# Weight words of the first three chunks made on GpSimd, and a written-out order for the first two groups of a float64-weight attention + MoE kernel

## The chip, the cores and the metric

One core of a Trainium2 chip. The metric is the device time of one execution in microseconds, as the median of several runs. Engines are named as in the profile: PE (TensorE matmul), PEld (its weight load), DVE (VectorE), ACT (ScalarE), POOL (GpSimd), SP (SyncE, which here issues the loads).

## The reference

```python
scores = scale * q @ k.T                      # 2 x 8 heads, 768 tokens, 64 wide
scores = scores - slopes * dist, masked to 8 global and 96 local keys
a = exp(scores - max) / (sum + 1e-9)
x = (a @ v) as 1536 x 512
h = x @ w_in                                  # 512 x 2048, float64 weights
g = where(h > 0, h, exp(min(h, 0)) - 1)
y = g @ w_out                                 # 2048 x 512
out = max(y @ w1, y @ w2, y @ w3) @ w_out2    # 512 x 768, 768 x 512
```

The weights arrive as float64, so each is a pair of 32-bit words. Matmuls run in fp32r, with each operand split in a high part and a rest; a product is three matmuls (high by high, high by rest, rest by high).

## The kernel before, in words

**Attention steps.** `Windowed` treats (256-token group, head pair, 128-token half) as a step k. A step's parts are spread over the engines: the load of q and k of a pair (`load_pair`, L190, SP), the product of q with its scale on POOL (`scale_queries`, L198, 128x256), the score matmuls (`scores_pe`, L228), bias and minimum on DVE (`scores_dve`, L254), the exponential on ACT (`scores_act`, L275), the sums (`sums`, L237), the reciprocal (`recip`, L266) and the norm (`norm`, L288: two DVE instructions a step, one per head), the transposes (`turn_pe`, L304, `turn_act`, L315), the product with v (`values_pe`, L327) and its split into high and rest (`values_high`, L337 on ACT, `values_low`, L343 on DVE).

**Prologue.** `windowed` runs steps 0 to 15 in a loop in which step k's scores stand beside the transposes of k-2 and the values of k-3. `FILL` puts idle matmuls on PE (L762) behind the scores of some steps. `WLOAD` says behind which steps a weight chunk (1 MB: one 128-column block of w_in and the matching rows of w_out) is loaded (L422, SP). From step 8 (`CONV`) on, a generator `convert` adds one piece of weight conversion a step. Steps 16 and 17 stand behind the loop, written out, with the second half of the first product between them (`half`).

**Conversion of a chunk** takes six passes over 128x1024 words: `c_rebase` (L457, ACT) scales the upper word as a float, `c_low` (L461, DVE) takes the lower word's top bits, two `c_word` (L468, DVE) join them to an fp32 word, `c_high` (L476, ACT) casts to fp32r, `c_rest` (L481, DVE) subtracts that from the word. `parts` gives the chunk's tile.

**Groups.** `run` then goes through three blocks of 512 tokens; in each, 16 groups fc: product h = x by w_in (`product`, L674), the ELU (L694, L695 on ACT, L699 on DVE), the split of its result (`high`, L681 ACT; `low`, L686 DVE), and the product with w_out of the group before (`out_high`, L705, `out_low`, L713). In the first block each group also carries an attention step of the second token block and the conversion of the chunks to come. Every engine works in the program's order (`manual_schedule`); waits are on semaphores only. Later, POOL also subtracts words for the second layer (`w_split`, L510), beside DVE's word passes there (`w_word`, L500).

Of the kernel before, what the change touches and what calls it, by code (L numbers as in the profile page):

```python
# [12 lines left out]
F32 = mybir.dt.float32  # L13
# [5 lines left out]
ALU = mybir.AluOpType  # L19
# [19 lines left out]
BLOCKS = [512, 512, 512]  # L39
CONV = 8  # L40
EARLY = 28
WARM = 10
FILL = {1: 2, 2: 2, 8: 2, 9: 2, 10: 2, 11: 2, 12: 2, 13: 2}
WLOAD = 2, 5, 9, 13
CHUNKS = [(c, i) for c in range(NCC) for i in range(3)]
BEHIND = [(c, i) for c in range(NCC) for i in (0, 2)] + [(c, 1) for c in range(NCC)]
# [352 lines left out]
class Feed:  # L399
# [45 lines left out]
        while self.nl <= min(a + (6 if self.nl < 2 * NFC else 2), 2 * NFC + 4 * NJ - 1):  # L445
            self.w_load()

    def parts(self, c):

        if c in self.whole:  # L450
            return [(self.whole[c], slice(0, 2))]
        return [(self.wraw[j], j % 2) for j in (2 * c, 2 * c + 1) if j in self.wraw and c < NFC]

    def c_rebase(self, c):
        for r, _ in self.parts(c):
            a = r[..., 1].bitcast(F32)
            self.nc.scalar.activation(a, a, AF.Copy, scale=2.0 ** -112)  # L457

    def c_low(self, c):
        for r, _ in self.parts(c):  # L460
            self.nc.vector.tensor_scalar(  # L461
                r[..., 0], r[..., 0], 29, 1, op0=ALU.logical_shift_right, op1=ALU.bitwise_or
            )

    def c_word(self, c, n):
        v, op = ((3, ALU.logical_shift_left), (0x80000000, ALU.bitwise_and))[n]
        for r, _ in self.parts(c):
            self.nc.vector.scalar_tensor_tensor(  # L468
                r[..., 0], r[..., 1], v, r[..., 0], op0=op, op1=ALU.bitwise_or
            )  # L470

    def c_high(self, c):
        for r, h in self.parts(c):
            if c not in self.w:
                self.w[c] = self.wt.tile([P, 2, 2, 512], F32R, tag="w", name="w")
            self.nc.scalar.copy(self.w[c][:, h, 0], r[..., 0].bitcast(F32))  # L476

    def c_rest(self, c):
        for r, h in self.parts(c):
            w = self.w[c]  # L480
            self.nc.vector.tensor_tensor(  # L481
                w[:, h, 1], r[..., 0].bitcast(F32), w[:, h, 0].bitcast(F32), op=ALU.subtract
            )
        for d, k in ((self.whole, c), (self.wraw, 2 * c), (self.wraw, 2 * c + 1)):
            if c < NFC:
                d.pop(k, None)
# [275 lines left out]
            self.nc.tensor.matmul(t[:, 0:P], z, z, start=True, stop=True)  # L762


    def run(self, at, k, x=None, h0=None, aside=None):

        nc, ps = self.nc, self.ps
        nblk = len(BLOCKS)  # L770
# [4 lines left out]
        ysave = {}  # L775
        left = None
        for bi, n in enumerate(BLOCKS):
            prev = y = None
            for fc in range(NFC):
                tag = ("h", "S0")[fc % 2] if k >= len(at.steps) + 2 else "h"  # L780
                if h0 is None:
                    h = ps.tile([P, 512], F32, tag=tag, name="h")[:, 0:n]
                    self.product(h, self.w[fc][:, 0], x, n, order=BEHIND if bi == 0 else None)
                else:
                    h, h0 = h0[:, 0:n], None
# [15 lines left out]
                if not late:  # L801
                    at.turn_act(k - 1, nc.vector.tensor_copy)
                    if k % 2 == 0:
                        at.pair_pe(k - 2)
                    at.scores_dve(k)
                    e = self.elu_exp(h, n)
                    at.scores_act(k)
                    if k % 2 == 0:
                        at.pair_out(k - 2, nc.scalar.copy)
                else:  # L810
                    ahead = bi == 0 and fc == NFC - 1
                    behind = joint and due and (ahead or k == len(at.steps))
                    if ahead:
                        at.scores_dve(k)
                        at.scores_act(k)
                        at.sums(k)
                        at.recip(k)
                        at.norm(k)
                    e = self.elu_exp(h, n)
                    if joint:  # L820
                        at.due_out(due, nc.scalar.copy)
                        if not behind:
                            at.turn_pe(k - 1)
                    if bi == fc == 0:
                        at.turn_act(k - 2, nc.scalar.copy)
# [4 lines left out]
                sooner = bi == 0 and (fc == 0 or k % 2)  # L830
                if sooner:
                    self.elu_max(e, h)
                if bi == 0 and not ahead:
# [22 lines left out]
                gl = self.low(e, gh, n)  # L856
# [9 lines left out]
                if late and bi:  # L866
# [1 line left out]
                    at.sums(k)  # L868
                    at.recip(k)
                    at.norm(k)  # L870
                if k % 2 == 0 and bi == fc == 0:
                    at.pair_pe(k - 2)
                    at.pair_out(k - 2, nc.scalar.copy)
                left = None
                if k % 2 == 1:
                    at.scale_queries(k // 2 + 1)
# [8 lines left out]
                if k % 2 == 0 and not joint and bi + fc:  # L885
                    at.pair_pe(k - 2)
                    at.pair_out(k - 2, nc.scalar.copy)
                if aside and bi == 1 and fc == 2:
# [293 lines left out]
def windowed(tc, ctx, io, flag):  # L1182
# [5 lines left out]
    with tc.manual_schedule():  # L1188
# [10 lines left out]
        x = f.split_tiles()  # L1199

        def convert():
            f.c_rebase(0)
            f.c_low(0)
            yield
            f.c_word(0, 0)
            f.c_rebase(1)
            yield
            f.c_word(0, 1)
            yield
            f.c_high(0)  # L1210
            f.c_low(1)
            yield
            f.c_rest(0)
            yield
            f.c_word(1, 0)
            yield

        words = convert()
# [2 lines left out]
        for k in range(first):  # L1221
            e = k % 2
            at.load_values(k, True)
            if e == 0:
                at.load_pair(k // 2 + 3, True)
                at.scale_queries(k // 2 + 1)
            at.scores_pe(k, (("S0", "S1"), ("y0", "y1"))[e])
            if k in FILL:
                f.fill(at.ident, FILL[k])
            at.turn_pe(k - 2, tags[k % 3])  # L1230
            at.values_pe(k - 3)
            if k >= first - 2:
                f.product(h, f.w[0][:, 0], x, GRP, 0, (k - first + 2) * 6, 6)
            at.scores_dve(k, True)
            at.turn_act(k - 2, nc.scalar.copy)
            at.scores_act(k)
            at.values_high(k - 3, x)
            at.sums(k)
            at.recip(k - 1)
            at.norm(k - 1)  # L1240
            at.values_low(k - 4, x)
            if k >= CONV:
                next(words, None)
            if k in WLOAD:
# [13 lines left out]
        at.turn_act(k - 2, nc.scalar.copy)  # L1258
        at.values_high(k - 3, x)
        at.values_low(k - 4, x)  # L1260
        at.scores_pe(k, m=2)
        at.turn_pe(k - 1, tags[(k + 1) % 3])
        at.scores_dve(k, True)
# [124 lines left out]
```

## Time and profile before

| | before |
|---|---|
| median of 3 runs (range) | 543.22 us (542.96 to 543.47) |
| profiled execution, its own time | 542.19 us |
| its span in the profile | 540.4 us |
| PE busy | 530.7 us (98%) |
| DVE busy | 393.7 us (73%) |
| ACT busy | 288.0 us (53%) |
| POOL busy | 82.9 us (15%) |

The span is the time from the first to the last instruction in the profile; the execution's own time also has what lies around it. Busy time of PE counts a matmul from its start to its modelled end, and matmuls overlap, so the share is no measure of the work done. Shares over the whole span hide that the kernel has stages with different limits: the first 60 us hold the prologue and the first groups, on which the change bears.

### The profile page before, as it was taken

The numbers are of one execution on the slowest core, as the hardware profiler recorded it, in microseconds if no ns is written. First come the engines' busy times: TensorE is split into PE (matmuls) and PEld (weight loads), VectorE is DVE, ScalarE is ACT, GpSimd is POOL, SyncE is SP. The second block draws the span as 40 slices with busy tenths as digits, with TensorE's granted clock in tenths as the row PEclk, the third lists the DMA queues.
The fourth block names the chain that finished last, engine by engine and source line by source line (L and its number), as shares of the span: only waits on it lengthen the run. The fifth ranks groups of instructions, "written<-read, shape, count | busy, mean of one in ns | idle before, by whom it ended". The sixth has DMA issues, their size and how long they took to land.

```text
span 540.4 us, 7751 instructions
## 1 busy us (share of the span) xinstructions
PE 530.7 (98%) x2746; PEld 426.8 (79%) x2746; DVE 393.7 (73%) x828; ACT 288.0 (53%) x649; POOL 82.9 (15%) x89
## 2 busy tenths in 40 slices
PE   8999999999999999999999999999999999999995
PEld 6667787777777888888888888888888888888884
DVE  6889999999854444443567656787886989779883
ACT  5979877888845555554545655552157321224020
POOL 4220000000000000000000044321034410335000
PEclk9999999999999999999999999999999999999999
DMA  8929055442310111000000031331029301876014
GB/s 284 397 95 409 21 196 196 156 161 83 101 46 24 45 44 44 21 19 1 0 2 0 1 117 40 116 115 42 1 71 308 146 1 40 270 293 234 1 73 168
DMA packets 23455, 59.21 MB, mean 110 GB/s; under 512 B 2416, under 2 KB 2416, under 8 KB 23408
## 3 DMA queue, kind: packets, MB, share of 16 engines
q1 hardware_dynamic: 18368, 49.46, 26.5%
q10 hardware_dynamic: 5040, 9.18, 4.5%
q8 instruction: 24, 0.39, 0.3%
q14 instruction: 23, 0.19, 0.1%
HBM read 49.19 MB, written 9.44 MB: 108 GB/s over the span
## 4 chain that ended last, share of the span: by engine, by line
PE 91%; DVE 5%; ACT 3%; issue 0%; POOL 0%; ACTq 0%; POOLq 0%
PE h L674 26%; PE y L705 16%; PE y L713 8%; PE y L975 8%; PE y L1069 5%; PE y L674 5%; PE S L975 4%; PE TX L327 3%; PE TX L304 3%; PE S L228 3%; PE S L1069 2%; PE TX L975 2%; PE S L674 2%; PE h L975 2%; PE TX L1069 2%; ACT p L275 1%
## 5 line engine op out<-in xcount | busy, mean ns | idle before, releaser
L674 PE MATMUL h<-xh,w 128*128 128x512 f32 (+1 forms) x432 | 122.2, 387 | 0.2 <-ACT w L476 0.2
L705 PE MATMUL y<-gh,w 128*128 128x512 f32 x384 | 98.7, 399 | 0.1
L510 POOL TENSOR_TENSOR w<-wr,w 128x512 fp32r<-128x512 f32 x42 | 62.9, 1507 | 231.8 <-ACT w L509 220.5
L674 PEld LDWEIGHTS h<-xh,w 128*128 128x128 f32 x432 | 80.2, 188 | 17.9 <-ACT w L476 0.8
L705 PEld LDWEIGHTS y<-gh,w 128*128 128x128 f32 x384 | 69.7, 188 | 14.3 <-issue 0.5
L674 PE MATMUL h<-xl,w 128*128 128x512 f32 (+1 forms) x216 | 71.0, 386 | 0.0
L699 DVE SCALAR_TENSOR_TENSOR e<-e,h 128x512 f32<-128x512 f32 x48 | 32.9, 685 | 49.5 <-ACT e L695 49.4
L509 ACT CAST w<-wr 128x512 fp32r<-128x512 f32 x42 | 27.6, 663 | 63.4 <-DVE wr L500 51.1
L694 ACT ACTIVATE e<-h 128x512 f32<-128x512 f32 x48 | 28.7, 599 | 55.3 <-PE h L674 51.2
L275 ACT ACTIVATE p<-p,m 128x232 f32<-128x232 f32 (+1 forms) x96 | 44.9, 471 | 17.1 <-DVE m L254 16.9
L713 PE MATMUL y<-gl,w 128*128 128x512 f32 x192 | 51.6, 390 | 0.0
L500 DVE SCALAR_TENSOR_TENSOR wr<-wr 128x512 uint32<-128x512 uint32 x48 | 44.2, 921 | 7.5 <-ACT wr L492 6.0
L686 DVE TENSOR_TENSOR gl<-e,gh 128x512 fp32r<-128x512 f32 x48 | 33.1, 689 | 19.9 <-ACT gh L681 19.9
L674 PEld LDWEIGHTS h<-xl,w 128*128 128x128 f32 x216 | 40.4, 188 | 8.1 <-issue 0.2
L198 POOL TENSOR_SCALAR raw<-raw,qsc 128x256 f32<-128x256 f32 x24 | 16.8, 699 | 193.4 <-DMA raw<-qk 193.4
L975 PE MATMUL y<-t,w 128*128 128x512 f32 x180 | 42.7, 389 | 0.0
L713 PEld LDWEIGHTS y<-gl,w 128*128 128x128 f32 x192 | 36.0, 188 | 8.0 <-issue 0.3
L681 ACT CAST gh<-e 128x512 fp32r<-128x512 f32 x48 | 29.6, 616 | 23.5 <-DVE e L699 23.3
L468 DVE SCALAR_TENSOR_TENSOR wr<-wr 128x1024 uint32<-128x1024 uint32 (+1 forms) x36 | 39.8, 1120 | 0.4
L975 PEld LDWEIGHTS y<-t,w 128*128 128x128 f32 x180 | 33.8, 188 | 7.0
L695 ACT ACTIVATE e<-e 128x512 f32<-128x512 f32 x48 | 30.3, 632 | 1.5
L985 ACT CAST g<-m 128x512 fp32r<-128x512 f32 x18 | 10.9, 621 | 35.2 <-DVE m L1004 27.0
(155 smaller groups left out, 837.5 us busy)
## 6 DMA issues: line engine op xcount, KB each, us to landing
wr<-wa SPq DMA_DIRECT2D x14, 1024.0 KB, 6.9
wr<-wb SPq DMA_DIRECT2D x24, 512.0 KB, 4.6
v<-v SPq DMA_DIRECT2D x24, 256.0 KB, 2.8
part<-row ACTq DMA_DIRECT2D x24, 256.0 KB, 4.6
raw<-qk SPq DMA_DIRECT2D x16, 312.0 KB, 4.6
row<-part SPq DMA_DIRECT2D x12, 256.0 KB, 3.1
out<-rows ACTq DMA_DIRECT2D x11, 256.0 KB, 2.3
raw<-qk SPq DMA_DIRECT2D x8, 260.0 KB, 4.7
```

What stands on the lines that cost most here:

```text
L275: self.nc.scalar.activation(p[:, o], p[:, o], AF.Exp, bias=m[:, u:u + 1], scale=-1.0, accum_out=m[:, 2 + u:3 + u],)
L468: self.nc.vector.scalar_tensor_tensor(r[..., 0], r[..., 1], v, r[..., 0], op0=op, op1=ALU.bitwise_or)
L500: self.nc.vector.scalar_tensor_tensor(t, a, c, t, op0=op, op1=ALU.bitwise_or)
L510: nc.gpsimd.tensor_tensor(w[:, u, 1], v, w[:, u, 0].bitcast(F32), op=ALU.subtract)
L674: nc.tensor.matmul(out[:, o:n], w[:, part % 2, c * P:c * P + P], (xl if part == 2 else xh)[:, c, o:n], start=(c, part) == order[0], stop=( ...
L686: (engine or self.nc.vector).tensor_tensor(gl[:, 0:n], e[:, 0:n], gh[:, 0:n].bitcast(F32), op=ALU.subtract)
L695: self.nc.scalar.activation(e, e, AF.Exp, scale=-1.0)
L699: self.nc.vector.scalar_tensor_tensor(e, e, -1.0, h, op0=ALU.add, op1=ALU.max)
L705: self.nc.tensor.matmul(y[e][:, 0:n], w[:, a, e * P:e * P + P], g[0][:, 0:n], start=fc == 0 and a == 0, stop=False,)
L713: self.nc.tensor.matmul(y[e][:, 0:n], w[:, 0, e * P:e * P + P], g[1][:, 0:n], start=False, stop=fc == NFC - 1,)
L975: self.nc.tensor.matmul(out, w[:, u, i % 2, b + c * P:b + c * P + P], o[:, i // 2, c], start=c == i == 0, stop=c == 1 and i == 2,)
L1069: nc.tensor.matmul(o, t[:, a, r], w[:, u, b], start=u == k == 0, stop=u == 1 and k == 2,)
```

## The change

- `c_early` is new: on POOL, it makes the bottom bits of a chunk (a multiplication of the lower word by 2^-29 with a cap of 7, in place of a shift and an OR of 1) and the rebased upper word (a multiplication by 2^-112). `POOLED = {5: 0, 8: 1, 14: 2}` puts it at the end of steps 5, 8 and 14, for chunks 0, 1 and 2. `c_rebase` and `c_low` of these chunks are gone.
- `convert` is reordered: step 8 has the first word pass of chunk 0, step 9 its second, step 10 its cast and the first word pass of chunk 1, step 11 the rest of chunk 0, steps 12 to 14 nothing, step 15 the second word pass of the first half of chunk 1. The other half, the two half casts and the first half rest of chunk 1 stand among steps 16 and 17.
- `FILL` has no entries for steps 12 and 13 any more (two instructions each).
- `begin` is new: the first two groups of `run` in a written-out order. `run` then starts at the third.

```diff
-FILL = {1: 2, 2: 2, 8: 2, 9: 2, 10: 2, 11: 2, 12: 2, 13: 2}
+FILL = {1: 2, 2: 2, 8: 2, 9: 2, 10: 2, 11: 2}
+POOLED = {5: 0, 8: 1, 14: 2}
...
+    def c_early(self, c):
+        for r, _ in self.parts(c):
+            a = r[..., 1].bitcast(F32)
+            self.nc.gpsimd.tensor_scalar(
+                r[..., 0], r[..., 0], 2.0 ** -29, 7.0, op0=ALU.mult, op1=ALU.min
+            )
+            self.nc.gpsimd.tensor_scalar(a, a, 2.0 ** -112, 1.0, op0=ALU.mult, op1=ALU.mult)
...
+    def begin(self, at, k, x, h):
+        copy, n = self.nc.scalar.copy, BLOCKS[0]
+        at.load_values(k)
+        self.w_ahead(4)
+        at.turn_pe(k - 2, "y2")
+        at.scores_pe(k, m=2)
+        at.recip(k - 1)
+        at.norm(k - 1)
+        at.turn_pe(k - 1)
+        e = self.elu_exp(h, n)
+        self.elu_max(e, h)
+        h = self.ps.tile([P, 512], F32, tag="h", name="h")
+        self.product(h, self.w[1][:, 0], x, n, order=BEHIND)
+        at.turn_act(k - 2, copy)
+        at.scores_dve(k)
+        self.c_rest(1, 1)
+        gh = self.high(e, n)
+        at.turn_act(k - 1, copy)
+        at.scores_act(k)
+        at.sums(k)
+        self.c_word(2, 0)
+        prev = gh, self.low(e, gh, n)
+        at.pair_pe(k - 2)
+        e = self.elu_exp(h, n)
+        self.c_word(2, 1)
+        self.elu_max(e, h)
+        at.pair_out(k - 2, copy)
+        self.c_high(2)
...
         def convert():
-            f.c_rebase(0)
-            f.c_low(0)
-            yield
             f.c_word(0, 0)
-            f.c_rebase(1)
             yield
             f.c_word(0, 1)
             yield
             f.c_high(0)
-            f.c_low(1)
+            f.c_word(1, 0)
             yield
             f.c_rest(0)
             yield
-            f.c_word(1, 0)
+            yield
+            yield
+            yield
+            f.c_word(1, 1, 0)
             yield
...
             if k in WLOAD:
                 f.w_load()
+            if k in POOLED:
+                f.c_early(POOLED[k])
...
+        f.c_word(1, 1, 1)
+        f.c_high(1, 0)
+        f.c_high(1, 1)
         at.scores_pe(k, m=2)
...
         at.values_low(k - 2, x)
+        f.c_rest(1, 0)
...
-        f.run(at, first + 2, x, h, lambda: covered(nc, at.const, ni, flag))
+        begun = f.begin(at, k + 2, x, h)
+        f.run(at, first + 4, x, begun, lambda: covered(nc, at.const, ni, flag))
```

POOL's queue from the set-up to the second layer, before (`raw` is a pair's q and k, `wr` a weight chunk, `w` its converted form):

```order
L110 MEMSET qsc 64x1 x8
masks.py:197 MEMSET ident 128x128
masks.py:199 AFFINE_SELECT ident<-ident 128x128
L198 TENSOR_SCALAR raw<-raw,qsc 128x256 x24
L510 TENSOR_TENSOR w<-wr,w 128x512 x42
```

and now:

```order
masks.py:199 AFFINE_SELECT ident<-ident 128x128
L199 TENSOR_SCALAR raw<-raw,qsc 128x256 x4
L460 TENSOR_SCALAR wr<-wr 128x1024
L463 TENSOR_SCALAR wr<-wr 128x1024
L199 TENSOR_SCALAR raw<-raw,qsc 128x256 x2
L460 TENSOR_SCALAR wr<-wr 128x1024
L463 TENSOR_SCALAR wr<-wr 128x1024
L199 TENSOR_SCALAR raw<-raw,qsc 128x256 x3
L460 TENSOR_SCALAR wr<-wr 128x1024
L463 TENSOR_SCALAR wr<-wr 128x1024
L199 TENSOR_SCALAR raw<-raw,qsc 128x256 x15
L523 TENSOR_TENSOR w<-wr,w 128x512 x42
```

Two passes over a chunk stand behind the products of pairs 0 to 3, two behind pairs 4 and 5, two behind pairs 6 to 8; the products of pairs 4, 6 and 9 now wait for them.

DVE in step 11, from its reciprocal to the scores of step 12 (`p` is a step's probabilities, `m` its small numbers, `xl` the rest of x), before:

```order
L266 RECIPROCAL m<-m 128x2
L288 TENSOR_SCALAR p<-p,m 128x232 x2
L343 TENSOR_TENSOR xl<-TX,xh 128x128
L461 TENSOR_SCALAR wr<-wr 128x1024
L254 ISA p,m<-S_475,rel 128x232
```

and now:

```order
L267 RECIPROCAL m<-m 128x2
L289 TENSOR_SCALAR p<-p,m 128x232 x2
L344 TENSOR_TENSOR xl<-TX,xh 128x128
L492 TENSOR_TENSOR w<-wr,w 128x2x512
L255 ISA p,m<-S_477,rel 128x232
```

The bottom bits of chunk 1 have left; the rest of chunk 0, which stood in step 12, has taken their place.

DVE in the first group, from the end of its scores on (`e` is the ELU's tile, `h` the product, `gl` the rest of the group's result), before:

```order
L461 TENSOR_SCALAR wr<-wr 128x1024
L481 TENSOR_TENSOR w<-wr,w 128x2x512
L266 RECIPROCAL m<-m 128x2
L288 TENSOR_SCALAR p<-p,m 128x232 x2
L686 TENSOR_TENSOR gl<-e,gh 128x512
L468 SCALAR_TENSOR_TENSOR wr<-wr 128x1024 x2
L699 SCALAR_TENSOR_TENSOR e<-e,h 128x512
```

and now:

```order
L492 TENSOR_TENSOR w<-wr,w 128x512
L479 SCALAR_TENSOR_TENSOR wr<-wr 128x1024
L699 TENSOR_TENSOR gl<-e,gh 128x512
L479 SCALAR_TENSOR_TENSOR wr<-wr 128x1024
L712 SCALAR_TENSOR_TENSOR e<-e,h 128x512
L267 RECIPROCAL m<-m 128x2
L289 TENSOR_SCALAR p<-p,m 128x232 x2
```

The bottom bits of chunk 2 and half of the rest of chunk 1 have left, and the norm now stands behind the second group's ELU.

## Rows read from the trace of the kernel before

**Rows 1.** Busy us by stretch: PE, PEld, DVE, ACT, POOL, clock, DMA share, GB/s

```profile
10.00:20.00 10.00, 8.77 (x78) 5.52 (x78) 8.08 (x46) 8.90 (x39) 1.43 (x3) 1.00 1.04 404
20.00:30.00 10.00, 9.73 (x83) 6.88 (x82) 9.86 (x38) 10.00 (x32) 2.31 (x4) 1.00 0.84 321
...
100.00:120.00 20.00, 20.00 (x106) 15.96 (x105) 19.07 (x39) 16.02 (x35) 0.48 (x1) 1.00 0.56 195
```

**Rows 2.** Timeline of PE, first groups: start, length, line, operation, [idle before <-ended by]

```profile
43.84 0.68 PE L304 MATMUL TX<-ident,p 128*116 128x128 f32 x4 [0.37 <-DVE p L288]
...
53.10 0.50 PE L674 MATMUL h<-xh,w 128*128 128x512 f32 x1 [0.21 <-ACT w L476]
```

**Rows 3.** Timeline of DVE, steps 5 to 8, same columns

```profile
13.55 0.48 DVE L288 TENSOR_SCALAR p<-p,m 128x128 f32<-128x128 f32 x2
...
14.39 0.29 DVE L254 CUSTOM_DVE_ANT_0 p<-S,rel 128x128 f32<-128x128 f32 x1 [0.16 <-PE S L228]
...
15.43 0.17 DVE L266 RECIPROCAL m<-m 128x2 f32<-128x2 f32 x1 [0.53 <-ACT m L237]
15.63 0.59 DVE L288 TENSOR_SCALAR p<-p,m 128x232 f32<-128x232 f32 x2
...
17.17 0.48 DVE L288 TENSOR_SCALAR p<-p,m 128x128 f32<-128x128 f32 x2
...
18.18 0.40 DVE L254 CUSTOM_DVE_ANT_0 p<-S,rel 128x232 f32<-128x232 f32 x1 [0.34 <-PE S L228]
...
19.95 0.69 DVE L461 TENSOR_SCALAR wr<-wr 128x1024 uint32<-128x1024 uint32 x1
```

**Rows 4.** Timeline of DVE, steps 9 to 15

```profile
22.09 1.22 DVE L468 SCALAR_TENSOR_TENSOR wr<-wr 128x1024 uint32<-128x1024 uint32 x1
...
24.05 0.59 DVE L288 TENSOR_SCALAR p<-p,m 128x232 f32<-128x232 f32 x2
...
29.65 1.22 DVE L481 TENSOR_TENSOR w<-wr,w 128x1024 fp32r<-128x1024 f32 x1
30.79 0.39 DVE L254 CUSTOM_DVE_ANT_0 p<-y,rel 128x232 f32<-128x232 f32 x1
...
33.46 0.39 DVE L254 CUSTOM_DVE_ANT_0 p<-S,rel 128x232 f32<-128x232 f32 x1
...
35.30 0.40 DVE L254 CUSTOM_DVE_ANT_0 p<-y,rel 128x232 f32<-128x232 f32 x1 [0.22 <-PE y L228]
```

**Rows 5.** Timeline of POOL, 0 to 60 us

```profile
1.67 0.14 POOL L86 IOTA rel<- 128x8 f32 x1
...
2.02 0.24 POOL L86 IOTA sc<- 128x128 f32 x1
...
10.02 0.48 POOL L198 TENSOR_SCALAR raw<-raw,qsc 128x256 f32<-128x256 f32 x1 [0.98 <-DMA raw<-qk]
...
24.37 0.62 POOL L198 TENSOR_SCALAR raw<-raw,qsc 128x256 f32<-128x256 f32 x1 [3.39 <-DMA raw<-qk]
...
29.83 1.38 POOL L198 TENSOR_SCALAR raw<-raw,qsc 128x256 f32<-128x256 f32 x1 [3.43 <-DMA raw<-qk]
```

**Rows 6.** Timelines of POOL and of DVE in the second layer, 399 to 412 us

```profile
399.82 5.05 POOL L510 TENSOR_TENSOR w<-wr,w 128x512 fp32r<-128x512 f32 x3 [18.69 <-ACT w L509]
399.82 2.41 DVE L500 SCALAR_TENSOR_TENSOR wr<-wr 128x512 uint32<-128x512 uint32 x2
...
409.61 1.42 DVE L500 SCALAR_TENSOR_TENSOR wr<-wr 128x512 uint32<-128x512 uint32 x2 [0.54 <-ACT wr L492]
```

**Rows 7.** Loads of chunks 0 and 1 (L422), each alone: issue, and time to landing

```profile
L422 SPq DMA_DIRECT2D wr<-wa x1: 652/652/652, 4.5 to 4.5; - x1
...
DMA to landing us min/median/max: 8.0/8.0/8.0
...
L422 SPq DMA_DIRECT2D wr<-wa x1: 557/557/557, 6.6 to 6.6; - x1
...
DMA to landing us min/median/max: 10.0/10.0/10.0
```

More of the change, by code (lines that the diff above doesn't have):

```diff
@@ L446, in w_ahead, with parts, c_rebase, c_low @@
             self.w_load()
-    def parts(self, c):
+    def parts(self, c, h=None):
+        hs = slice(0, 2) if h is None else slice(h, h + 1)
         if c in self.whole:
-            return [(self.whole[c], slice(0, 2))]
+            return [(self.whole[c][:, hs], hs)]
         return [(self.wraw[j], j % 2) for j in (2 * c, 2 * c + 1) if j in self.wraw and c < NFC]
-    def c_rebase(self, c):
+    def c_early(self, c):
         for r, _ in self.parts(c):
             a = r[..., 1].bitcast(F32)
+            self.nc.gpsimd.tensor_scalar(
+                r[..., 0], r[..., 0], 2.0 ** -29, 7.0, op0=ALU.mult, op1=ALU.min
+            )
+            self.nc.gpsimd.tensor_scalar(a, a, 2.0 ** -112, 1.0, op0=ALU.mult, op1=ALU.mult)
+    def c_rebase(self, c, h=None):
+        for r, _ in self.parts(c, h):
+            a = r[..., 1].bitcast(F32)
             self.nc.scalar.activation(a, a, AF.Copy, scale=2.0 ** -112)
-    def c_low(self, c):
-        for r, _ in self.parts(c):
+    def c_low(self, c, h=None):
+        for r, _ in self.parts(c, h):
             self.nc.vector.tensor_scalar(
@@ L463, in c_low, with c_word @@
             )
-    def c_word(self, c, n):
+    def c_word(self, c, n, h=None):
         v, op = ((3, ALU.logical_shift_left), (0x80000000, ALU.bitwise_and))[n]
-        for r, _ in self.parts(c):
+        for r, _ in self.parts(c, h):
             self.nc.vector.scalar_tensor_tensor(
@@ L470, in c_word, with c_high, c_rest @@
             )
-    def c_high(self, c):
-        for r, h in self.parts(c):
+    def c_high(self, c, h=None):
+        for r, hs in self.parts(c, h):
             if c not in self.w:
                 self.w[c] = self.wt.tile([P, 2, 2, 512], F32R, tag="w", name="w")
-            self.nc.scalar.copy(self.w[c][:, h, 0], r[..., 0].bitcast(F32))
-    def c_rest(self, c):
-        for r, h in self.parts(c):
+            self.nc.scalar.copy(self.w[c][:, hs, 0], r[..., 0].bitcast(F32))
+    def c_rest(self, c, h=None):
+        for r, hs in self.parts(c, h):
             w = self.w[c]
             self.nc.vector.tensor_tensor(
-                w[:, h, 1], r[..., 0].bitcast(F32), w[:, h, 0].bitcast(F32), op=ALU.subtract
+                w[:, hs, 1], r[..., 0].bitcast(F32), w[:, hs, 0].bitcast(F32), op=ALU.subtract
             )
+        if h == 0:
+            return
         for d, k in ((self.whole, c), (self.wraw, 2 * c), (self.wraw, 2 * c + 1)):
@@ L762, in fill, with run @@
             self.nc.tensor.matmul(t[:, 0:P], z, z, start=True, stop=True)
-    def run(self, at, k, x=None, h0=None, aside=None):
+    def begin(self, at, k, x, h):
[26 more added lines that the diff above has]
+        self.c_high(2)
+        y = self.out_tiles()
+        self.out_high(y, 0, prev, n)
+        self.out_low(y, 0, prev, n)
+        at.recip(k)
+        at.norm(k)
+        gh = self.high(e, n)
+        self.c_rebase(3)
+        self.c_rest(2)
+        gl = self.low(e, gh, n)
+        k += 1
+        at.turn_pe(k - 1)
+        at.turn_act(k - 1, copy)
+        at.scale_queries(k // 2 + 1)
+        at.load_pair(k // 2 + 2)
+        self.w_ahead(6)
+        at.scores_dve(k)
+        at.scores_act(k)
+        at.sums(k)
+        self.c_low(3)
+        self.c_word(3, 0)
+        at.recip(k)
+        at.norm(k)
+        return y, (gh, gl)
+    def run(self, at, k, x=None, begun=None, aside=None):
         nc, ps = self.nc, self.ps
@@ L777, in run @@
         for bi, n in enumerate(BLOCKS):
-            prev = y = None
-            for fc in range(NFC):
+            y, prev = begun or (None, None)
+            for fc in range(2 if begun else 0, NFC):
                 tag = ("h", "S0")[fc % 2] if k >= len(at.steps) + 2 else "h"
[L781 to L785, printed above, removed]
+                h = ps.tile([P, 512], F32, tag=tag, name="h")[:, 0:n]
+                self.product(h, self.w[fc][:, 0], x, n, order=BEHIND if bi == 0 else None)
                 at.load_values(k)
@@ L823, in run @@
                             at.turn_pe(k - 1)
-                    if bi == fc == 0:
-                        at.turn_act(k - 2, nc.scalar.copy)
                     if not due:
@@ L829, in run @@
                     next(sums, None)
-                sooner = bi == 0 and (fc == 0 or k % 2)
+                sooner = bi == 0 and k % 2
                 if sooner:
@@ L870, in run @@
                     at.norm(k)
-                if k % 2 == 0 and bi == fc == 0:
-                    at.pair_pe(k - 2)
-                    at.pair_out(k - 2, nc.scalar.copy)
                 left = None
@@ L884, in run @@
                     at.turn_act(k - 1, nc.scalar.copy)
-                if k % 2 == 0 and not joint and bi + fc:
+                if k % 2 == 0 and not joint:
                     at.pair_pe(k - 2)
@@ L901, in run @@
                 prev = gh, gl
+            begun = None
             if bi + 1 < nblk:
@@ L1281, in windowed @@
         at.norm(k)
-        at.turn_pe(k, tags[k % 3])
-        at.recip(k + 1)
-        at.norm(k + 1)
         for _ in words:
             pass
-        f.run(at, first + 2, x, h, lambda: covered(nc, at.const, ni, flag))
+        begun = f.begin(at, k + 2, x, h)
+        f.run(at, first + 4, x, begun, lambda: covered(nc, at.const, ni, flag))
 def build(tc, io):
```

## The prediction
> **What bounds the kernel now.** I read the busy times by stretch first [rows 1]. PE shows 20.00 us of 20 between 100 and 120 us, but a PE row also counts waiting inside the pipeline, so the share of PE alone says little; what says more is that PE's own timeline has next to no gaps once the first groups are over, while its last two gaps stand at 43.84 us (0.37 us, ended by DVE's norm) and at 53.10 us (0.21 us, ended by ACT's cast of the third weight chunk) [rows 2]. From 53 us on the kernel runs at PE's rate. Whatever the change wins or loses must therefore be won or lost ahead of that point, and it then stays to the end.
>
> Ahead of it the limit is another one. Between 20 and 30 us DVE is busy 9.86 of 10 us and ACT 10.00, against 8.08 and 8.90 in the ten before [rows 1]. Read DVE's own order there: in steps 4 to 8 it has small waits (0.16 us at 14.39, 0.53 at 15.43, 0.34 at 18.18) [rows 3]; from step 9 to step 14 there are none, and a step lasts as long as its work on DVE: 2.67 us from the scores of step 13 (30.79) to those of step 14 (33.46), with a 1.22 us pass in it, and 1.84 us from there to 35.30, with none [rows 4]. So in this stretch a microsecond of DVE is a microsecond of the kernel.
>
> **What the change takes off DVE and ACT.** DVE loses the bottom-bit pass of chunks 0, 1 and 2 (0.69 us at 19.95 [rows 3]); ACT loses the three rebasing passes. By steps: step 8 has a word pass (1.22 us [rows 4]) where the bottom-bit pass stood, +0.53 us; steps 9 and 10 keep their word pass; step 11 has the rest of chunk 0 (1.22 us) where a bottom-bit pass stood, +0.53; steps 12 and 13 have none, so each falls from 2.67 to the 1.84 us of step 14, -0.83 each. Sum: 0.53 + 0.53 - 1.66 = -0.60 us. The new half passes of chunk 1 behind step 15 I cost at nothing, since DVE waits there for sums and scores; if that cover is gone they cost up to 1.9 us (three halves of 1.22). The two idle gaps of PE in the first groups go too, because chunk 1 is cast before the first group and the norm of the last step no longer stands behind as much: -0.58 us [rows 2]. PE's own work in the two groups is the same, in another order. The four matmuls that are no longer filled in lie on PE while DVE is the limit: nothing. SP's order is unchanged. Without anything else the change would win 0.60 + 0.58 = 1.18 us.
>
> **What it puts on POOL.** Six passes over 128x1024. No row of before shows one, so I bound it. POOL's product over 128x256 takes 0.48 us [rows 5]. Four of them give 1.92 us, the upper end. An IOTA of 128 columns takes 0.24 us and one of 8 takes 0.14, which is 0.83 ns a column; 0.48 + 768 x 0.83 ns = 1.12 us is the lower end. When the same product starts while a DVE pass is under way it ends 0.34 us after that pass: the row at 29.83 ends at 31.21, the DVE pass of 29.65 at 30.87 [rows 4, 5]. So 0.14 us of it is start-up and 0.34 the part that shuts out DVE, and scaling that part gives 0.14 + 4 x 0.34 = 1.50 us. I take 1.30, between the lower end and 1.50, since both are scaled from rows as near as there are: 0.14 of start-up and **1.16 us of hold**.
>
> "Hold" is the point. At 29.83 POOL waited for DVE; the other way round DVE waits for POOL. At 409.61 two DVE word passes of 128x512 take 1.42 us, and at 399.82 the same two take 2.41, with three POOL passes in flight back to back: POOL got in between the two of them, and the second stood for about a microsecond [rows 6]. The scores are spared: at 30.79 they take 0.39 us [rows 4], with the POOL product of 29.83 still under way. So the norm of each step, two DVE instructions, and the weight passes are what POOL will shut out. The Trainium skill says the same as a rule (SBUF — State Buffer, section "Who interferes with whom"): GpSimd and DVE share one pair of ports, whichever starts first has it for its whole instruction, and a DVE instruction with at most one SBUF input and outside the two-port mode is exempt. That rule speaks against the change; without it the sum would be the 1.18 us won.
>
> **The walk.** Chunk 0 lands at 4.5 + 8.0 = 12.5 us, chunk 1 at 6.6 + 10.0 = 16.6 [rows 7].
> Chunk 0: the first pass holds from 12.7 to 13.85. The norm due at 13.55 [rows 3] has its first half 0.30 us late; the second POOL pass, queued by then, gets in between the halves and holds 1.16 us. The norm ends 1.46 us late; the waits of 0.16 and 0.53 us behind it [rows 3] take up 0.69. Left: +0.77.
> Chunk 1: POOL does the products of pairs 4 and 5 first and asks at 16.74; the norm of 15.63, now 16.40 to 17.0, has its second half started by then, so the pass holds from 17.0 to 18.16. The norm of 17.17, now due at 17.94, waits 0.22 us, and the second pass costs its second half 1.16: +1.38. The wait of 0.34 at 18.18 is used up: +1.04. Sum at step 8: +1.81. With step 8's longer pass: +2.34.
> Chunk 2: pair 8 lands as before (24.37 is ended by a DMA [rows 5]), its product slips in behind the word pass of step 9, and the first POOL pass holds from about 26.1 to 27.3. The norm of 24.05 [rows 4], now due at 26.39, loses 0.90 and then 1.16 us: +2.06. Sum: +4.40.
> Then +0.53 at step 11 and -1.66 in steps 12 and 13: the scores of step 14 start 3.27 us late. Behind step 14 the chain is the same and moves as a whole; the gaps of the first groups give back 0.58. **Sum: +2.7 us.** The profiled execution took 542.19 us, 1.03 below the median of the three runs (543.22); 542.19 + 2.7 = 544.9, and against the median **545.9 us**.
> Six holds enter, so 0.1 us more on each is some 0.6 us. At a pass of 1.12 us the sum is 2.7 - 1.1 = +1.6 (544.8), at 1.50 us +3.9 (547.1), at 1.92 us +6.4 (549.6).
> The Trainium skill (GPSIMD Engine Reference, section "Elementwise — side-by-side cycle accounting") puts a short loop body at 1.03 cycles an element, which at 1.2 GHz would make the hold an estimated 0.88 us and the sum +1.0 us; no run here shows a pass of this size.
>
> **The rivals.**
> *The holds hide.* The six passes fall beside scores, POOL waits for DVE more often than DVE for POOL, and what is left is the -1.18 us: 542.0 us. For it: the scores, two of 0.39 us in each step [rows 4], are exempt, and DVE's waits of steps 4 to 8 can take up part of a delay [rows 3]. Against it: norms recur every two microseconds or so [rows 3] and each POOL pair is 2.6 us long, so a norm falls into each. It decides if fewer than two of the six holds are met in full. Chance 0.27.
> *The two sides cancel.* Half of the hold is met, for instance because POOL does not get in between the halves of a norm: three times 1.16 us less, 2.7 - 3.5 = -0.8, or two times, +0.4: 542.4 to 543.6 us. Chance 0.13.
> *POOL is slower than I take it.* With integers to convert, 1.92 us or more. Then the products of pairs 4 and 5 queue behind the chunk passes as well, and PE's scores of step 8 wait for POOL itself; before, that of pair 4 ran at 10.02 [rows 5], long ahead of the scores of step 8 at 18.18. 549.6 us or more. For it: no row has an integer pass on POOL. Chance 0.08.
> The forecast, passes of 1.1 to 1.8 us that mostly meet a norm: 0.52.
>
> **How the numbers follow.** A measurement here tells about 0.2% (1.1 us) from no change. Slower by more: 0.52 + 0.08 = 0.60; within: 0.13; faster by more: 0.27. Forecast 545.9. The likeliest case alone spans 544.8 to 549.0; the range reaches down over the cancelling case to just below the 542.0 of hidden holds: 541.7 to 549.0, which leaves out the slow-POOL case and a part of the fast one.
>
> **What would show it.** Right: six POOL passes of 1.2 to 1.5 us beginning at 12.5, 17 and 26; norms of over 1.5 us (now 0.48 to 0.59) where they fall; scores of step 8 near 20.0 instead of 18.18, of step 14 near 36.7 instead of 33.46; no gap of PE between the end of the first product and the third. Wrong: norms at their old length while POOL is busy, or POOL passes well below a microsecond. A granted clock below 1.00 [rows 1] anywhere ahead of 60 us would add time that I don't count, since PE stands idle longer there and four filling matmuls are gone.

## The result, and the profile after

| | before | after |
|---|---|---|
| median of 6 runs each (range) | 543.03 us (542.45 to 543.47) | 548.73 us (547.56 to 550.57) |
| profiled execution, its own time | 542.19 us | 548.62 us |
| its span | 540.4 us | 546.8 us |

The changed kernel takes 1.0108 times as long, with an interval of 1.0098 to 1.0118: slower by 5.7 us, where 2.7 were forecast. The sign is as forecast and the time lies in the range, at its upper end (548.73 of 549.0); the size is a little over twice the forecast. Between the two profiled executions the difference is 6.43 us, and it is this one that is followed below. The busy times of the whole span, first line of the page after:

```profile
PE 532.6 (97%) x2738; PEld 427.6 (78%) x2738; DVE 398.2 (73%) x827; ACT 285.4 (52%) x647; POOL 97.9 (18%) x95
```

DVE has one instruction fewer than before (828) and is busy 4.5 us longer (393.7 before). Busy by stretch, the columns as in [rows 1]:

```profile
10.00:20.00 10.00, 7.42 (x64) 4.58 (x64) 8.47 (x38) 7.50 (x34) 7.71 (x5) 1.00 1.04 406
20.00:30.00 10.00, 7.13 (x58) 4.66 (x56) 9.76 (x25) 6.29 (x26) 9.78 (x7) 1.00 0.86 292
30.00:40.00 10.00, 8.75 (x52) 5.57 (x52) 8.39 (x31) 6.09 (x22) 3.07 (x4) 0.66 0.21 70
40.00:50.00 10.00, 9.91 (x91) 7.49 (x90) 8.32 (x37) 8.69 (x31) 0.05 (x1) 1.00 0.36 128
```

Two things are to be seen. Between 20 and 30 us DVE is as full as before (9.76 us against 9.86) with 25 instructions instead of 38: each takes longer. And between 30 and 40 us PE has a granted clock of 0.66, where every stretch of before has 1.00. POOL's own timeline after (start, length, line, operation, [idle before]):

```profile
12.13 3.88 POOL L460 TENSOR_SCALAR wr<-wr 128x1024 uint32<-128x1024 uint32 x1 [3.74 <-DMA wr<-wa]
16.08 1.11 POOL L463 TENSOR_SCALAR wr<-wr 128x1024 f32<-128x1024 f32 x1
17.17 0.97 POOL L199 TENSOR_SCALAR raw<-raw,qsc 128x256 f32<-128x256 f32 x2
18.22 3.91 POOL L460 TENSOR_SCALAR wr<-wr 128x1024 uint32<-128x1024 uint32 x1
22.20 1.12 POOL L463 TENSOR_SCALAR wr<-wr 128x1024 f32<-128x1024 f32 x1
...
25.82 3.75 POOL L460 TENSOR_SCALAR wr<-wr 128x1024 uint32<-128x1024 uint32 x1
29.64 1.11 POOL L463 TENSOR_SCALAR wr<-wr 128x1024 f32<-128x1024 f32 x1
```

The float pass takes 1.11 us, the lower bound of the forecast. The integer pass takes 3.75 to 3.91, twice the upper bound. So chunk 1's first pass starts at 18.22, where 17.0 was forecast, and its two passes last until 23.32, long past the scores of step 8 (19.76). DVE's timeline after, steps 4 to 15:

```profile
12.19 1.42 DVE L289 TENSOR_SCALAR p<-p,m 128x232 f32<-128x232 f32 x2
...
14.56 0.48 DVE L289 TENSOR_SCALAR p<-p,m 128x128 f32<-128x128 f32 x2
...
15.40 0.29 DVE L255 CUSTOM_DVE_ANT_0 p<-S,rel 128x128 f32<-128x128 f32 x1 [0.17 <-PE S L229]
...
16.44 0.17 DVE L267 RECIPROCAL m<-m 128x2 f32<-128x2 f32 x1 [0.52 <-ACT m L238]
16.64 1.16 DVE L289 TENSOR_SCALAR p<-p,m 128x232 f32<-128x232 f32 x2
...
18.74 0.88 DVE L289 TENSOR_SCALAR p<-p,m 128x128 f32<-128x128 f32 x2
...
19.76 0.40 DVE L255 CUSTOM_DVE_ANT_0 p<-S,rel 128x232 f32<-128x232 f32 x1
...
20.82 1.45 DVE L289 TENSOR_SCALAR p<-p,m 128x232 f32<-128x232 f32 x2
...
22.39 2.00 DVE L479 SCALAR_TENSOR_TENSOR wr<-wr 128x1024 uint32<-128x1024 uint32 x1
...
25.98 2.02 DVE L479 SCALAR_TENSOR_TENSOR wr<-wr 128x1024 uint32<-128x1024 uint32 x1
...
28.75 2.13 DVE L289 TENSOR_SCALAR p<-p,m 128x232 f32<-128x232 f32 x2
...
32.22 0.39 DVE L255 CUSTOM_DVE_ANT_0 p<-y,rel 128x232 f32<-128x232 f32 x1
...
34.88 0.39 DVE L255 CUSTOM_DVE_ANT_0 p<-S,rel 128x232 f32<-128x232 f32 x1
...
37.22 0.40 DVE L255 CUSTOM_DVE_ANT_0 p<-y,rel 128x232 f32<-128x232 f32 x1 [0.71 <-PE y L229]
...
39.65 0.40 DVE L255 CUSTOM_DVE_ANT_0 p<-S,rel 128x232 f32<-128x232 f32 x1 [0.79 <-PE S L229]
...
42.31 0.40 DVE L255 CUSTOM_DVE_ANT_0 p<-y,rel 128x232 f32<-128x232 f32 x1 [1.04 <-PE y L229]
```

Norms of 0.59 or 0.48 us [rows 3, 4] take 0.88 to 2.13, word passes of 1.22 take 2.0, and the scores keep their 0.40. Call **shut-out** what DVE's norms and weight passes between 11 and 45 us take beyond their usual length. Summed over this timeline it is 6.00 us, in eleven instructions: 1.81 ahead of the scores of step 8 (19.76), 4.19 behind them.

PE waits for DVE meanwhile. PE's timeline after:

```profile
31.14 0.65 PE L305 MATMUL y<-ident,p 128*116 128x128 f32 x4 [2.55 <-DVE xl L344]
31.72 1.08 PE L328 MATMUL y<-p,v 116*64 116x128 f32 x8
...
40.13 0.66 PE L328 MATMUL y<-p,v 116*64 116x128 f32 x8
...
48.21 0.51 PE L687 MATMUL h<-xh,w 128*128 128x256 f32 x2
...
52.15 0.50 PE L687 MATMUL h<-xh,w 128*128 128x512 f32 x1
...
59.34 0.48 PE L687 MATMUL h<-xh,w 128*128 128x512 f32 x1
...
157.68 1.52 PE L687 MATMUL h<-xh,w 128*128 128x512 f32 x6
```

Behind the idle 2.55 us the same eight matmuls take 1.08 us that take 0.66 at 40.13: PE is at the lower of its two levels (1.2 of 2.4 GHz) for some microseconds. The three rows ahead of the last, with no idle time shown before them, are the second half of the first product (41.20 before), the second product (46.48) and the third (53.10, [rows 2]); the last row is the first product of the second token block. DVE's scores of steps 11 and 12 and PE's places before, to compare with:

```profile
25.98 0.39 DVE L254 CUSTOM_DVE_ANT_0 p<-y,rel 128x232 f32<-128x232 f32 x1
...
28.11 0.39 DVE L254 CUSTOM_DVE_ANT_0 p<-S,rel 128x232 f32<-128x232 f32 x1
...
41.20 0.50 PE L674 MATMUL h<-xh,w 128*128 128x256 f32 x2
...
151.55 1.52 PE L674 MATMUL h<-xh,w 128*128 128x512 f32 x6
```

How late the changed kernel is, the profiled executions compared (start after minus start before), beside the forecast's walk:

| place | forecast | measured |
|---|---|---|
| scores of step 8 | +1.81 | +1.58 (19.76 - 18.18) |
| scores of step 11 | +4.40 | +6.24 (32.22 - 25.98) |
| scores of step 12 | +4.93 | +6.77 (34.88 - 28.11) |
| scores of step 14 | +3.27 | +6.19 (39.65 - 33.46) |
| scores of step 15 | +3.27 | +7.01 (42.31 - 35.30) |
| third product | +2.7 | +6.24 (59.34 - 53.10) |
| first product of the second token block | +2.7 | +6.13 (157.68 - 151.55) |

### The profile page after: what moved, and what is told of

Same layout as the page of the kernel before. It is cut to its first block, busy times and chain, and to the rows that moved or that the text cites. A ratio compares the mean times of both kernels' runs of the same rounds, so it can differ in the third digit from the quotient of the medians.

```text
span 546.8 us, 7743 instructions
## 1 busy us (share of the span) xinstructions
PE 532.6 (97%) x2738; PEld 427.6 (78%) x2738; DVE 398.2 (73%) x827; ACT 285.4 (52%) x647; POOL 97.9 (18%) x95
## 4 chain that ended last, share of the span: by engine, by line
PE 92%; DVE 3%; ACT 2%; DMA 2%; issue 0%; SPq 0%; POOL 0%; ACTq 0%; POOLq 0%
PE h L687 26%; PE y L718 16%; PE y L726 8%; PE y L1035 7%; PE y L1129 4%; PE y L687 4%; PE S L1035 4%; PE TX L328 3%; PE TX L305 3%; PE S L229 3%; PE TX L1035 2%; PE S L1129 2%; PE S L687 2%; PE h L1035 2%; DMA wr<-wa 2%; PE TX L1129 1%
## 5 line engine op out<-in xcount | busy, mean ns | idle before, releaser
L479 DVE SCALAR_TENSOR_TENSOR wr<-wr 128x1024 uint32<-128x1024 uint32 (+1 forms) x37 | 41.8, 1144 | 0.4
L289 DVE TENSOR_SCALAR p<-p,m 128x232 f32<-128x232 f32 (+1 forms) x96 | 32.2, 378 | 1.7
```

Source lines behind the costliest of these rows:

```text
L289: nc.vector.tensor_scalar(p[:, o], p[:, o], m[:, 6 + u:7 + u], None, op0=ALU.mult)
L479: self.nc.vector.scalar_tensor_tensor(r[..., 0], r[..., 1], v, r[..., 0], op0=op, op1=ALU.bitwise_or)
```

## The experiments

Two questions: which part of the change costs the time, and why it costs more than forecast. "Late" below is a run's start of the second half of the first product against before (41.20 us); "at the second block" is the same for the first product of the second token block (151.55).

| run | POOL's passes a chunk | shut-out | late | at the second block | time against before |
|---|---|---|---|---|---|
| after | integer, float | 6.00 | +7.01 | +6.13 | 1.0108 [1.0098, 1.0118] |
| e1_no_pool | none | 0.00 | +1.52 | +0.66 | 1.0003 [0.9990, 1.0016] |
| e2_float_on_pool | float | 1.32 | +4.20 | +3.29 | 1.0042 [1.0022, 1.0062] |
| e3_int_on_pool | integer | 2.75 | +3.86 | +2.94 | 1.0070 [1.0044, 1.0096] |
| e4_pool_alone | integer, float; order of before | 5.17 | +2.76 | +2.56 | 1.0051 [1.0033, 1.0068] |
| e7_order_alone | none; passes at their old places | 0.41 | +0.53 | -0.33 | 0.9978 [0.9969, 0.9987] |
| e8_half_passes | integer, float, in halves | 1.82 | +2.12 | +1.28 | 1.0040 [1.0022, 1.0058] |
| e10_fill_wide | integer, float; more filling | 6.38 | +6.22 | +5.33 | 1.0080 [1.0060, 1.0100] |
| e11_two_float | two floats | 4.30 | +6.08 | +5.24 | 1.0083 [1.0061, 1.0106] |

**1. Without POOL (e1).** The two passes go back to DVE and ACT, at the places where the change calls them.

```diff
     def c_early(self, c):
...
-            self.nc.gpsimd.tensor_scalar(
-                r[..., 0], r[..., 0], 2.0 ** -29, 7.0, op0=ALU.mult, op1=ALU.min
+            self.nc.vector.tensor_scalar(
+                r[..., 0], r[..., 0], 29, 1, op0=ALU.logical_shift_right, op1=ALU.bitwise_or
             )
-            self.nc.gpsimd.tensor_scalar(a, a, 2.0 ** -112, 1.0, op0=ALU.mult, op1=ALU.mult)
+            self.nc.scalar.activation(a, a, AF.Copy, scale=2.0 ** -112)
```

> The changed kernel with the two early passes of each chunk on DVE (shift and OR, 0.69 us) and ACT (1.15 us) at the same places, none on POOL. Theory H (POOL's passes shut DVE out: DVE instructions between 12 and 33 us are 6.0 us longer than free ones in the changed kernel): all of that goes, DVE gets 3 x 0.69 back, of which the one behind step 5 falls into waits; 542.0 to 543.5 us, granted clock 1.00 between 30 and 40 us. Theory O (the new order of pieces and of the first two groups is what costs): stays at 547 to 549 us.

543.09 us, no difference from before; no shut-out. Without POOL's passes the new order costs nothing. (How much they cost in the order of before is asked in experiment 3.)

**2. One pass each (e2, e3).** e2 leaves only the float pass on POOL, e3 only the integer one; the other goes where e1 has it.

> The changed kernel with only the float pass (1.11 us) on POOL; bottom bits on DVE. H: three holds of about 1 us, of which each meets a norm or a weight pass for some 0.6 us, and 3 x 0.69 us more of DVE: 543.5 to 545.5 us. O: 547 to 549 us. If the float passes were the larger part of the loss: over 546.5 us.

> The changed kernel with only the integer pass (3.9 us) on POOL; rebasing on ACT. H: six holds of some 0.9 us (one near the start, one near the end of each pass): 545 to 547.5 us, more than with the float pass alone. If what counts is not the hold but that POOL is late with the products of pairs 4, 6 and 9: near the changed kernel, 547.5 to 549 us, with PE waiting for POOL in the scores.

545.6 us, at the upper edge of what was expected, and 546.06 us. Each alone shuts DVE out, and together they do so by more (6.00 us) than the sum of both alone (1.32 + 2.75). Their times don't add up as cleanly: both have stretches at a low granted clock (0.74 and 0.75 between 10 and 30 us in e2, 0.83 between 20 and 30 in e3).

**3. POOL's passes in the order of before (e4).** Everything of the change is undone but `c_early` and `POOLED`; `c_rebase` and `c_low` return for pooled chunks without doing anything.

```diff
+    def c_early(self, c):
+        self.pooled.add(c)
...
     def c_low(self, c):
+        if c in self.pooled:
+            return
```

> The kernel before with its own order, only the bottom bits and rebasing of chunks 0 to 2 moved to POOL at steps 5, 8 and 14. H: 6 us of holds less 3 x 0.69 us of DVE: 546 to 550 us. O: no loss from POOL, 541 to 543 us.

545.67 us, just below the 546 to 550 expected; the shut-out is 5.17 us, less than in the change (6.00). (Behind the norm of 14.39 the rest of x and the first scores stand too, but at the same time as its second half; they are not counted again.) POOL alone explains about 2.4 us of the 5.7. Late by 2.76 us: 5.17 less the two bottom-bit passes that before has ahead of this place (2 x 0.69) is 3.8, so in this order 1.0 us of the shut-out is hidden. Its clock is 1.00 in every stretch from 10 to 50 us.

The other 3.3 us of the 5.7 come only where POOL's passes and the new order meet. Experiment 5 puts about 1.2 of them down to the clock. Of the rest the traces show this much: in the change both word passes of steps 8 and 9 stand (2.00 and 2.02 us), in e4 neither does (1.30 and 1.21), since one starts after chunk 1's passes and the other falls in the middle of chunk 2's integer pass. How the rest divides was not followed. POOL and DVE at that other word pass, in e4:

```profile
25.63 3.83 POOL L460 TENSOR_SCALAR wr<-wr 128x1024 uint32<-128x1024 uint32 x1
...
27.30 1.21 DVE L483 SCALAR_TENSOR_TENSOR wr<-wr 128x1024 uint32<-128x1024 uint32 x1
```

**4. The new first groups alone (e7).** Nothing on POOL; the rebasing and bottom-bit passes of chunks 0 and 1 at their places of before, chunk 2's rebasing at step 13, its bottom bits in `begin` behind the scores. The first word pass of chunk 1 is back at its old step too, so what remains of the new order is the split of chunk 1's last passes, `begin`, and the filling taken out behind steps 12 and 13.

```diff
-POOLED = {5: 0, 8: 1, 14: 2}
...
         at.scores_dve(k)
+        self.c_low(2)
         self.c_rest(1, 1)
...
         def convert():
+            f.c_rebase(0)
+            f.c_low(0)
+            yield
             f.c_word(0, 0)
+            f.c_rebase(1)
...
             f.c_high(0)
-            f.c_word(1, 0)
+            f.c_low(1)
...
-            yield
+            f.c_word(1, 0)
...
-            if k in POOLED:
-                f.c_early(POOLED[k])
+            if k == 13:
+                f.c_rebase(2)
```

> Nothing on POOL: bottom bits on DVE and rebasing on ACT at the places of the kernel before (the rebasing of chunk 2 at step 13, its bottom bits in the first group), with the changed kernel's split of chunk 1's last passes and its written-out first two groups. H: the first product starts as early as before and the gaps of the first groups stay closed (in the changed kernel and in the one without POOL passes that gave back 0.9 us between the first product and the fourth): 542.0 to 542.7 us, a ratio of 0.998 to 0.9995. O: 543.5 us or more. This is also the version that could beat both.

541.98 us (541.52 to 542.36, 11 runs): 1.2 us faster than before, and the fastest version here. Its page and PE's timeline, the second and the third product:

```profile
PE 529.8 (98%) x2738; PEld 426.4 (79%) x2738; DVE 394.2 (73%) x830; ACT 287.9 (53%) x650; POOL 81.7 (15%) x89
...
45.67 0.50 PE L677 MATMUL h<-xh,w 128*128 128x512 f32 x1
...
52.85 0.48 PE L677 MATMUL h<-xh,w 128*128 128x512 f32 x1
```

From the second half of the first product (41.73) to the third is 11.12 us, against 11.90 before: both gaps of [rows 2] are gone. The profiled executions differ by only 0.2 us, since that of before (542.19) lies 0.98 below its median in this comparison (543.17); where before's other runs spend that microsecond, no trace shows.

**5. The clock (e5, e10, e9).** e5 and e10 leave the change as it is and put more idle matmuls behind the scores; e9 takes e7 and removes most of them.

```diff
-FILL = {1: 2, 2: 2, 8: 2, 9: 2, 10: 2, 11: 2}
+FILL = {1: 2, 2: 2, 8: 2, 9: 2, 10: 5, 11: 8, 12: 2, 13: 2}
```

```diff
-FILL = {1: 2, 2: 2, 8: 2, 9: 2, 10: 2, 11: 2}
+FILL = {1: 2, 2: 2, 3: 2, 4: 2, 5: 4, 6: 2, 7: 4, 8: 4, 9: 4, 10: 5, 11: 7, 12: 3, 13: 2}
```

```diff
-FILL = {1: 2, 2: 2, 8: 2, 9: 2, 10: 2, 11: 2}
+FILL = {1: 2, 2: 2}
```

> The changed kernel with more filling matmuls (5 behind step 10, 8 behind step 11, 2 each behind 12 and 13), so that PE has work in the gaps ahead of 32 us. Theory C (a good part of the loss is the lower granted clock, 0.66 in 30 to 40 us): clock 1.00 there and 546.5 to 547.5 us. H: the clock may stay up, but DVE's excess of 6 us stays, so at most 1 us less: 547.7 us or more.

e5 decides nothing: 547.39 us (1.0089 [1.0073, 1.0104]) with a clock of 1.00 between 30 and 40 us, but the clock fell at another place, to 0.70 between 10 and 20 us.

> The changed kernel with filling matmuls behind every step from 3 to 13 (2 to 7 each), to hold the granted clock up while POOL's passes stay as they are. Within the runs so far 0.001 of mean clock goes with 0.22 to 0.4 us, and no run of the changed kernel was above 0.992. Theory H+C: with the clock at 0.997 or more the time is 546 to 547.2 us, the holds alone; DVE's excess stays near 6 us. H alone (the clock is only a sign of waiting): 548 to 549 us even with the clock up. If the clock does not come up, the run says nothing on the price.

In e10 the clock is up from 10 to 60 us, with DVE shut out as before. Its stretches, columns as in [rows 1]:

```profile
20.00:30.00 10.00, 9.83 (x84) 7.66 (x82) 9.79 (x26) 6.22 (x28) 9.85 (x6) 1.00 0.78 279
30.00:40.00 10.00, 8.28 (x73) 5.54 (x71) 9.47 (x36) 7.17 (x25) 2.55 (x5) 1.00 0.27 91
```

547.56 us, 1.2 less than after (548.73), and between what the two theories expected (546 to 547.2, 548 to 549). So the low clock is worth about 1.2 of the 5.7 us, 0.8 of them between the profiled executions (at the second block +5.33 against +6.13). The intervals of the two kernels just touch (up to 1.0100 here, from 1.0098 for after), so the size is rough. The other 4.5 stand with the clock at 1.00.

> The kernel with the new order alone and nothing on POOL, without the filling matmuls behind steps 8 to 11. It asks for the clock by itself. C: the granted clock falls below 1.00 somewhere between 10 and 40 us, and the kernel takes 1 to 3 us more than with them. H: DVE sets the pace there, so slower matmuls cost little: within 0.7 us of the one with the fillings, whether the clock falls or not.

542.35 us, 0.9988 [0.9977, 1.0000]: at most a few tenths more than e7, with a clock of 1.00 from 10 to 40 us of its profile. In one of its runs the mean clock was 0.991, and that took 544.57 us; one at 0.999 took 541.63. What the filling changes is how often such a run occurs, if anything; ten runs don't settle it.

**6. Shorter passes (e8).** Each POOL pass is split in two of 128x512.

```diff
-        for r, _ in self.parts(c):
+        for r, _ in self.parts(c, 0) + self.parts(c, 1):
```

> The changed kernel with each POOL pass cut in two of 128x512 (twelve instead of six). H: a meeting costs DVE half as much (0.45 instead of 0.9 us), while there are more of them; DVE's excess falls from 6.0 to 3.5 to 5 us: 546.5 to 548 us. If what counts is POOL's total time: no change or slower, 548.5 to 550 us.

544.65 us, 4.1 less than after and well below the 546.5 to 548 expected; the shut-out falls from 6.00 to 1.82 us, where 3.5 to 5 were expected. Its clock is 1.00 in every stretch from 10 to 60 us of its profile, so what the low clock costs in the change is part of the 4.1. POOL's timeline, and one row of PE's:

```profile
12.50 2.13 POOL L460 TENSOR_SCALAR wr<-wr 128x512 uint32<-128x512 uint32 x1 [3.79 <-DMA wr<-wa]
14.70 0.67 POOL L463 TENSOR_SCALAR wr<-wr 128x512 f32<-128x512 f32 x1
...
27.12 2.86 POOL L460 TENSOR_SCALAR wr<-wr 128x512 uint32<-128x512 uint32 x1
...
18.70 0.66 PE L229 MATMUL S<-raw 64*128 64x232 f32 x4 [0.91 <-POOL raw L199]
```

POOL's work is the same or a little longer (2 x 2.0 us or more against 3.9). What falls is the single hold, to 0.41 us at most (0.92 in the change); and here it is POOL that waits at times (2.86 us at 27.12). The row of PE shows a price of its own: the scores of step 8 wait 0.91 us for the product of pair 4, which stands on POOL behind four half passes.

**7. No integers, the same number of passes (e11).** The bottom bits go to DVE, as in e1, and POOL makes two float passes (2^-56 twice) a chunk.

```diff
+            for _ in range(2):
+                self.nc.gpsimd.tensor_scalar(a, a, 2.0 ** -56, 1.0, op0=ALU.mult, op1=ALU.mult)
```

> Two float passes of 1.1 us on POOL per chunk (the upper word scaled by 2^-56 twice), bottom bits on DVE: six passes of the length that the forecast took, instead of one float and one integer pass. If the step of the forecast that failed is the integer pass (3.9 us, holding twice): 544 to 545.5 us, at most 1.5 us above the kernel with one float pass at the same clock. If the walk over holds itself is off: 547 us or more.

A miss: 547.75 us, though POOL's passes are down to 1.1 to 1.4 us each. That is the time expected if the walk over the holds is off, and not the length of the pass. POOL's timeline, and DVE's at the first pair:

```profile
12.12 2.28 POOL L464 TENSOR_SCALAR wr<-wr 128x1024 f32<-128x1024 f32 x2 [3.50 <-DMA wr<-wa]
...
12.11 2.42 DVE L289 TENSOR_SCALAR p<-p,m 128x232 f32<-128x232 f32 x2
```

Both halves of the norm stand: the norm takes 2.42 us where the change has 1.42. Two short passes back to back shut DVE out by more there than one integer pass of 3.88 us; the shut-out is 4.30 us, that of e2's single float pass 1.32. The clock was low here too (0.71 between 10 and 20 us), so the time itself is no clean measure of the holds. By the shut-out, the length of the integer pass is not by itself what makes the change slow.

## Why the prediction was right in its sign and half in its size

**Right: what decides.** POOL's passes shut DVE out of norms and word passes, and the scores are spared. Without them the loss is gone (e1), each has its part (e2, e3), and in the order of before they alone make the kernel slower (e4), though by 2.4 us of the 5.7 only. The Trainium skill's rule (SBUF — State Buffer, section "Who interferes with whom") says that whichever of DVE and GpSimd issues first has the shared pair for the whole instruction and the other is blocked. The trace agrees that they shut each other out, but not for the whole instruction: the norm at 14.56 takes its usual 0.48 us inside POOL's pass of 12.13 to 16.01.

**Mis-sized: the pass.** "I take 1.30" holds for neither: the float pass takes 1.11 us, the integer pass 3.75 to 3.91. Even so, the shut-out to step 8 was smaller than forecast, 1.81 us against 0.30 + 1.16 + 0.22 + 1.16 = 2.84.

**Failed: "the waits ... take up 0.69".** They took nothing: DVE still waits 0.17 us at 15.40 and 0.52 at 16.44, as it did at 14.39 and 15.43 [rows 3]. Such a wait is part of the step's own chain (scores, exponential, sums, reciprocal) and moves with the delay. Only the 0.34 at 18.18 was used up. That +1.81 came out near the measured +1.58 is luck: two errors that cancel, and 0.18 us that the changed kernel is late ahead of POOL's first pass (norm at 12.19 against 12.01), for a reason not followed.

**Failed: chunk 1 done by step 8.** Behind the scores of step 8 the forecast had 2.06 us of shut-out, all chunk 2's. Measured are 4.19. Chunk 1's integer pass lasts from 18.22 to 22.13 and its float pass to 23.32, and so they still held the norm of step 8 (1.45 us, +0.86) and the word pass (2.00, +0.78); chunk 2's held the word pass of step 9 (2.02, +0.80) and both halves of the norm at 28.75 (2.13, +1.54). With the two longer steps as forecast (0.53 + 0.53) that is 5.25, and from step 8 to step 12 the kernel lost 6.77 - 1.58 = 5.19. This is the largest part of what was missed, 2.1 us.

**Missed: steps 12 and 13 give back 1.66.** They gave back 0.58. PE ran at the lower clock there, and DVE waited for it (0.71 and 0.79 us at 37.22 and 39.65). In e10, at full clock, the same stretch gives back 1.8 (step 12 at 35.3, step 14 at 38.9; 28.1 and 33.5 before). The last sentence of the prediction named such a clock as time it didn't count; it was to be counted, since the forecast itself made PE idle there.

**Failed: "behind step 14 the chain is the same and moves as a whole".** From step 14 to step 15 it lost another 0.82 us. With steps 12 and 13 free of passes DVE reaches step 15 before PE, which needs 2.67 us for a step there. e1 shows it without any hold, at clock 1.00. DVE's timeline and PE's in e1:

```profile
34.15 0.40 DVE L255 CUSTOM_DVE_ANT_0 p<-S,rel 128x232 f32<-128x232 f32 x1 [0.44 <-PE S L229]
...
36.82 0.40 DVE L255 CUSTOM_DVE_ANT_0 p<-y,rel 128x232 f32<-128x232 f32 x1 [0.43 <-PE y L229]
...
34.05 0.65 PE L305 MATMUL y<-ident,p 128*116 128x128 f32 x4
...
36.72 0.65 PE L305 MATMUL TX<-ident,p 128*116 128x128 f32 x4
```

From step 14 to step 15 e1 takes 36.82 - 34.15 = 2.67 us, before 1.84. So the 1.66 us won in steps 12 and 13 were worth half. The half passes of chunk 1 behind step 15, costed at nothing, did cost nothing: the first product is as late as step 15 (+7.01).

**Right, a little small: the gaps of the first groups.** 0.58 us forecast, 7.01 - 6.13 = 0.88 measured; e7 keeps 0.86 (+0.53 to -0.33), and that is what its trace gains.

Sum of the profiled executions at the second block: 1.58 + 5.19 - 0.58 + 0.82 - 0.88 = +6.13. The forecast has 1.81 + 3.12 - 1.66 + 0 - 0.58 = +2.7 for the same five terms: the 3.4 us between them are the second (2.1), the third (1.1) and the fourth (0.8), less 0.5 in the two others. The other 0.3 us to the 6.43 of the whole fall behind it and weren't followed.

**The rivals.** Hidden holds and the cancelling case fell: norms and word passes stood. The slow-POOL rival had the pass right (beyond 1.92 us) and its mechanism wrong: it had PE's scores of step 8 wait for POOL's products, but the scores of step 8 came behind no such wait of PE or DVE (19.76). Only e8 shows that wait (0.91 us). The loss is still by shutting out DVE; that this rival's 549.6 us lies nearer to the 548.73 than the forecast does is luck.

## What to carry to other kernels

Before work is moved from a full DVE to GpSimd, count which of DVE's other instructions its passes will meet: here 2.07 us of DVE's work went and 6.00 us of standing came. If it must go there, cut it in short instructions (e8: 1.82 us of standing for the same work, though even so the kernel is 0.4% slower than before), and don't price an integer pass by a float one. A new order is to be tried without the moved work too: e7 is the one version that gains. A wait on the delayed chain absorbs nothing, a step made shorter on one engine is worth only what the next engine allows, and where a forecast makes PE idle, its clock belongs in the sum.

## What the runs showed of the hardware

- On POOL a multiplication with a cap on 128x1024 uint32 takes 3.75 to 3.91 us, two multiplications on as many floats 1.11 or 1.12; on 128x512 they take about 2.0 and 0.67 where DVE doesn't hold them up (e8).
- The integer pass does not hold DVE throughout. In the pass of 12.13 to 16.01 the first norm stands 0.83 us, while the norm at 14.56 runs in its usual 0.48. In that of 25.82 to 29.57 the word pass begun at 25.98 stands 0.80 and the norm at 28.75 stands again (0.62 in its first half). In e4 a whole word pass (27.30, 1.21 us) runs unhindered in the middle of the pass of 25.63. So it holds near its start and near its end and is free between. Why was not tried.
- Two POOL passes back to back get in between DVE's instructions one by one (e11's norm of 2.42 us).
- The granted clock does not follow from the longest gap of PE alone. Behind a gap of 1.72 us ahead of 14.10 (e2) and one of 1.20 ahead of 14.10 (e5) it fell to 0.74 and 0.70; behind 1.40 ahead of 13.96 (after), 1.19 ahead of 13.79 (e4) and 1.46 ahead of 31.57 (e10) it stayed at 1.00. Runs of one kernel differ by it: of e1's ten, those at a mean clock of 0.990 and 0.995 took 545.85 and 544.62 us, the others (0.997 to 0.999) 542.62 to 543.45.
